# Top-k attention with a squared-ReLU feed-forward: scores laid out with 512 columns in each outer PSUM bank, and half of the pair maxima moved to another bank

## The chip, the cores and the metric

The kernel runs on one core of one Trainium2 chip. A core has a matrix engine (TensorE, "PE" in the profile; its weight loads are listed as "PEld"), a vector engine (VectorE, "DVE"), a scalar engine (ScalarE, "ACT"), a general engine (GpSimd, "POOL") and a queue that issues transfers (SyncE, "SP"). Each engine works through its own list of instructions in order, and the engines wait for one another through semaphores. Matrix products land in PSUM, which this kernel treats as eight banks of 512 fp32 columns on 128 partitions; everything else lies in SBUF.

The metric is device time in microseconds (us): the median over the executions of the program. Lower is better.

## The reference

There are 8 batches of 8 heads; each head has 576 queries and 576 keys of 64 numbers. For every query only the 32 largest scores count. The attention output of all heads, 4608 rows of 512 numbers, then goes through two matrices with a squared ReLU between.

```python
scores = scale * np.matmul(q, k.transpose(0, 1, 3, 2))        # scale = 1/8
kth = np.partition(scores, -top_k, axis=-1)[..., -top_k:-top_k + 1]
scores = np.where(scores >= kth, scores, -1000000000.0)
attn = np.exp(scores - np.max(scores, axis=-1, keepdims=True))
attn = attn / (np.sum(attn, axis=-1, keepdims=True) + 1e-09)
attn_out = np.matmul(attn, v)
x = attn_out.transpose(0, 2, 1, 3).reshape(B * S, H * D)      # 4608 x 512
out = np.maximum(x @ w_in, 0.0) ** 2 @ w_out                  # 512 -> 2048 -> 512
```

## The kernel before

**Blocks.** Two heads form a pair, 32 pairs in all. A *block* is the score table of 128 queries for both heads of a pair: 128 partitions by 2 x 576 columns. A pair has four such blocks, and the last 64 queries of two pairs share a fifth one (the Z block, in which one head's queries lie on partitions 0 to 63 and the other's on 64 to 127). That makes 144 blocks. Each goes through this pipeline, in which some four blocks are under way at a time:

1. *Loads and transposes*, once per pair (`load_pair`). q and k come in by three transfers each (lines 444 and 446), are transposed by PE, and ACT copies them from PSUM into the tile `qk`: 512 columns of q (line 484), 512 of k (line 485), and the remaining 64 of both in one instruction (line 486). In `qk` head 0 of the pair lies on partitions 0 to 63 and head 1 on 64 to 127.
2. *Scores* (`scores`, `scores_z`). The products are fp32. Head 0 uses rows 0 to 63 of the PE array and head 1 rows 64 to 127, so that products of the two can run side by side. Each product is done in two passes, which the profile lists as two matmuls. The 1152 columns of a block lie without a gap in banks 0, 1 and 2: head 0 takes columns 0 to 575, head 1 takes 576 to 1151. [...] head 0 needs products of 512 and 64 columns, and head 1 of 448 and 128. Head 0's 64 columns and head 1's 448 share bank 1; a semaphore (`fence`) keeps the second of them until the first is done.
3. *Copy.* ACT copies the whole block to SBUF, to the tile `st` (line 532).
4. *Pair maxima.* Each row of 576 scores is folded in halves: `m` holds the larger of each pair of scores that lie 288 apart. DVE makes it in two instructions, each taking one operand from PSUM and the other from `st`: `m1` (line 595) for the second half of the pairs, which it writes into PSUM, and `m0` (line 597) for the first half, which goes to SBUF. ACT copies m1's result into `m` (`mc`, line 599). DVE then folds `m` once more into `f` (`big`, line 601), with one operand in PSUM again. POOL makes the smaller members of the pairs by integer sums and differences (line 583).
5. *Selection* (DVE). Rounds of "eight largest" (MAX8, lines 624 and 631) and "strike these out" (MATCH_REPLACE8, line 628) give the 32nd largest score of each row, `kth`.
6. *Mask and probabilities.* ACT turns scores below `kth` into a weight `w` (line 639). In `attend`, PE transposes the nine 128-column parts of a block and adds a steep multiple of `w` to each (`flip`, recorded at the helpers' lines 428 and 425), in a group of four and a group of five; the result `e` takes banks 3, 4 and the first 128 columns of bank 5. One ACT instruction over all three banks makes the exponentials (line 672).
7. *Attention output* (`collect`) and *feed-forward* (`feed`), which uses banks 6 and 7 in turn, as do the transposes of step 1 and the output of step 7.

**Where the pair maxima lie.** m1 writes its 288 columns into columns 128 to 415 of bank 2, beside head 1's last 128 score columns. The scores of the next block begin with a product that covers bank 2, so the plan lets them start only when both the score area (`ss`) and this quarter (`sq`) are free. `ss` comes free after m1, m0 and the copy of line 532; `sq` comes free after `big`, which is its last reader:

```python
pl.op("pe", 1.25 if gi != Z else 1.4, tg - LEAD, scores if gi != Z else scores_z, r=qu,
      w=[ss] + ([sq] if M1 else []), take=[ss, st] + ([sq] if M1 else []))
```

There is one `ss`, one `sq` and one `e` (pools `ps_s`, `ps_q`, `ps_e`, one slot each).

**The order of the work.** Nothing is ordered by hand. The host program describes every operation with an engine, an assumed duration, a priority and its tiles (`Plan.op`); `Plan.schedule` plays the engines through with these durations and gives each free engine the ready operation with the lowest priority number whose tiles are free. The lists that come out are fixed in the program. The constants PER, LEAD, ME, MQ, MP, MA, LAG, STEP, LATE and LAGL are parts of those priorities: PER is the assumed distance of two blocks, LEAD how far ahead scores are made, ME, MQ, MA and MP how early m1/m0, `big`, `mc` and the POOL steps are placed, LAG and LAGL how late the feed-forward is. SQ sets which squares go to POOL and which to ACT (`i * SQ % 8 < SQ`). A tile of a pool is given out in the order in which the tiles were described, except for `psum`, which gives to whoever asks first.

Of the kernel before, what the change touches and what calls it, by code (L numbers as in the profile page):

```python
# [12 lines left out]
P = 128  # L13
# [7 lines left out]
class Pool:  # L21


    def __init__(self, name, n):
        self.name, self.n = name, n
        self.free = list(range(n))
        self.last = [None] * n
        self.made = self.taken = 0

    def take(self, tl):  # L30
        if self.name != "psum" and tl.num != self.taken:
            return None
        s = self.find(tl.width)
        if s is not None:
            self.taken += 1
        return s
# [255 lines left out]
def bass_top_k_attn__then__act_relu_squared_kernel(  # L292
# [11 lines left out]
    REST = (512, 0)  # L304
    NHP = 4
# [8 lines left out]
    def sb(name, shape, dt=FP32, n=None):  # L314
# [4 lines left out]
    PER = 5.5  # L319
    T0 = 12.0  # L320
    LEAD = 25.86
    ME = 12.62
    MQ = 12.73
    MP = 5.72
    MA = 14.76
    SQ = 5.43
    M1 = 1
    LAG = 7.32
    STEP = 3.3
    LATE = 1.21  # L330
    LAGL = 18.31
    WARM = 0
# [22 lines left out]
        "qk": ([P, 2, S], FP32, 5), "vb": ([P, 12, D + 1], BF16, 5),  # L355
# [17 lines left out]
    ps_s, ps_q, ps_e, psum = Pool("ps_s", 1), Pool("ps_q", 1), Pool("ps_e", 1), Pool("psum", 2)  # L373
    BASE = {"ps_s": 0, "ps_q": 2, "ps_e": 3, "psum": 6}
# [13 lines left out]
    def wide(t):  # L388

        b = BASE[t.pool.name]  # L390
        return ps32[:, b:b + 3, :].rearrange("p b c -> p (b c)")[:, 0:2 * S]
# [38 lines left out]
    def build(full, weights, pl):  # L430
# [7 lines left out]
        def load_pair(b, hp, base):  # L438
            rq, rk, rv = tile("rq"), tile("rk"), tile("rv")

            def load(t, src, queue=nc.sync):
                def fn():
                    r = at(t)
                    res = [queue.dma_start(r[:, 0:4, h, :], src[b, 2 * hp + h, 0:512, :].rearrange(
                        "(tb p) d -> p tb d", p=P)) for h in range(2)]
                    res.append(queue.dma_start(
                        r[0:64, 4, :, :], src[b, 2 * hp:2 * hp + 2, 512:576, :].rearrange("h p d -> p h d")))
                    return res
                return fn
# [10 lines left out]
            pl.op("sp", 2.3, base - 80, load(rq, q), w=[rq], take=[rq], sem=slot_sem, ndma=3)  # L460
            via = "act" if not full and not state["pairs"] else None
            state["pairs"] += 1
            pl.op("sp", 2.3, base - 79.9, load(rk, k, nc.scalar if via else nc.sync), w=[rk], take=[rk], sem=slot_sem,
# [12 lines left out]
            def t5():  # L476
# [7 lines left out]
            pl.op("act", .6, base - 42.5, lambda: act.copy(at(qk)[:, 0, 0:512], bank(tq)), r=[tq], w=[qk])  # L484
            pl.op("act", .6, base - 42.4, lambda: act.copy(at(qk)[:, 1, 0:512], bank(tk)), r=[tk], w=[qk])
            pl.op("act", .3, base - 42.3, lambda: act.copy(
                at(qk)[:, :, 512:576], bank(tx)[:, 0:128].rearrange("p (a c) -> p a c", a=2)), r=[tx], w=[qk])
# [4 lines left out]
        def top_k(gi, qks, tg):  # L492
# [6 lines left out]

            def scores():  # L500
                o = wide(ss)
                for h, to, c0, n_ in ((0, 512, 512, 64), (1, 1024, 448, 128), (0, 0, 0, 512), (1, 576, 0, 448)):
                    x = at(qks[h])
                    if to == 576:
                        pe.wait_ge(fence, fences[0])
                    ins = mm(o[:, to:to + n_], x[64 * h:64 * h + 64, 0, 128 * gi:128 * gi + 128],
                             x[64 * h:64 * h + 64, 1, c0:c0 + n_], to != 576)
                    if to == 512:
                        fences[0] += 1
                        ins.then_inc(fence, 1)  # L510
                return ins


            def scores_z():
                o = wide(ss)
                for i, runs in ((0, [((512, 512, 64), (0, 0, 512)), ((512, 0, 64), (0, 64, 512))]),
                                (1, [((1024, 384, 128), (576, 512, 64), (640, 0, 384)),
                                     ((1024, 448, 128), (576, 0, 448))])):
                    x = at(qks[i])
                    for k_ in range(3):  # L520
                        for h in range(2):
                            if k_ < len(runs[h]):
                                to, c0, n_ = runs[h][k_]
                                ins = mm(o[64 * h:64 * h + 64, to:to + n_], x[64 * h:64 * h + 64, 0, 512:576],
                                         x[64 * h:64 * h + 64, 1, c0:c0 + n_], not 576 <= to < 1024)
                return ins

            qu = sorted(set(qks), key=lambda t: t.num)
            pl.op("pe", 1.25 if gi != Z else 1.4, tg - LEAD, scores if gi != Z else scores_z, r=qu,
                  w=[ss] + ([sq] if M1 else []), take=[ss, st] + ([sq] if M1 else []))  # L530

            cp = [pl.op("act", 1.2, tg - LEAD + 1, lambda: act.copy(  # L532
                at(st)[:, :, :].rearrange("p i c -> p (i c)"), wide(ss)), r=[ss], w=[st])]
# [44 lines left out]
            else:  # L578
# [7 lines left out]
                def parts(a, n_):  # L586

                    return two(wide(ss)[:, a:], S, n_), at(st)[:, :, HALF + a:HALF + a + n_]

                def quarter():  # L590
                    return two(ps32[:, 2, 128:416], QUART, QUART)

                if M1:

                    m1 = dve(.36, lambda: vec.tensor_tensor(quarter(), *parts(QUART, QUART), ALU.max), dp=-ME,  # L595
                             r=[ss], hold=[st, sq], after=cp)
                    m0 = dve(.36, lambda: vec.tensor_tensor(at(m)[:, :, 0:QUART], *parts(0, QUART), ALU.max), dp=-ME,  # L597
                             r=[ss], hold=[st], after=cp, w=[m], take=[m])
                    mc = pl.op("act", .45, tg - MA, lambda: act.copy(at(m)[:, :, QUART:HALF], quarter()), hold=[sq],  # L599
                               w=[m], after=[m1, m0])  # L600
                    big = dve(.36, lambda: vec.tensor_tensor(  # L601
                        at(f)[:, :, 0:QUART], at(m)[:, :, 0:QUART], quarter(), ALU.max), dp=-MQ,
                        hold=[m, sq], after=[m0, mc], w=[f], take=[f])
                else:
                    dve(.67, lambda: vec.tensor_tensor(at(m)[:, :, :], *parts(0, HALF), ALU.max), dp=-ME,
                        r=[ss], hold=[st], after=cp, w=[m], take=[m])
                    big = dve(.67, lambda: vec.tensor_reduce(
                        at(f)[:, :, 0:QUART], at(m)[:, :, :].rearrange("p i (a c) -> p i c a", a=2), AX.X, ALU.max),
                        dp=-MQ, r=[m], w=[f], take=[f])
# [45 lines left out]
        def attend(gi, st, wt, tt):  # L655

            e, pt = Tile(ps_e), tile("p")

            def flip(cols, i0):
                sf, wf = (at(t)[:, :, :].rearrange("p i c -> p (i c)") for t in (st, wt))  # L660
                outs = [(wide(e)[:, 128 * (i0 + i):128 * (i0 + i) + 128], c, (i0 + i) % 4 == 0)
# [9 lines left out]
            pl.op("pe", .84, tt + .1, lambda: flip([640, 768, 896, 1024, 512], 4), r=[st, wt], w=[e], order=[o_t])  # L671
            pl.op("act", 1.15, tt + 1, lambda: act.activation(  # L672
                at(pt)[:, :, :].rearrange("p k q -> p (k q)"), wide(e), ACTF.Exp, scale=0.125), r=[e], w=[pt])
# [317 lines left out]
```

## Time and profile before

| | us |
|---|---|
| median of 3 runs (lowest to highest) | 902.43 (901.22 to 904.34) |
| the profiled execution, its own time | 901.76 |
| its span, from the first to the last instruction | 900.0 |
| DVE busy | 830.1 (92% of the span) |
| PE busy | 832.0 (92%) |
| POOL busy | 799.7 (89%) |
| ACT busy | 751.9 (84%) |

A busy engine's time is a union: overlapping instructions are counted once. The durations of single DVE and PE instructions overlap their neighbours, so means times counts exceed the busy time. In a line of instruction groups the figures are: busy us and mean ns of one instruction, then the engine's idle time just before these instructions and what ended most of it. In a list of waits they are: total us, number of waits, longest. In a table of windows each engine has its busy us and its number of instructions, then come the share of full clock that PE was granted, and the share and rate of the DMA engines.

### The profile page before, as it was taken

The numbers are of one execution on the slowest core, as the hardware profiler recorded it, in microseconds if no ns is written. First come the engines' busy times: TensorE is split into PE (matmuls) and PEld (weight loads), VectorE is DVE, ScalarE is ACT, GpSimd is POOL, SyncE is SP. The second block draws the span as 40 slices with busy tenths as digits, with TensorE's granted clock in tenths as the row PEclk, the third lists the DMA queues.
The fourth block names the chain that finished last, engine by engine and source line by source line (L and its number), as shares of the span: only waits on it lengthen the run. The fifth ranks groups of instructions, "written<-read, shape, count | busy, mean of one in ns | idle before, by whom it ended". The sixth has DMA issues, their size and how long they took to land.

```text
span 900.0 us, 21960 instructions
## 1 busy us (share of the span) xinstructions
PE 832.0 (92%) x7810; PEld 598.2 (66%) x7810; DVE 830.1 (92%) x3409; ACT 751.9 (84%) x1210; POOL 799.7 (89%) x833
## 2 busy tenths in 40 slices
PE   5777778999999999998999999999899999999996
PEld 3555556676767666766677657676667676776774
DVE  2988899999999999999999999999999999999961
ACT  3767687898989898989889989898989898888872
POOL 6988898999999899988999999997899999999961
PEclk8988799999999999999999999999999999999999
DMA  6632551101310322012110123202221120000101
GB/s 135 165 109 83 133 117 38 54 9 43 82 39 15 73 71 64 20 39 66 28 52 16 28 63 88 61 13 53 53 57 38 39 54 15 25 2 25 24 14 40
DMA packets 126967, 48.18 MB, mean 54 GB/s; under 512 B 119168, under 2 KB 119168, under 8 KB 126848
## 3 DMA queue, kind: packets, MB, share of 16 engines
q1 hardware_dynamic: 125648, 46.39, 20.6%
q8 instruction: 63, 1.03, 0.5%
q14 instruction: 56, 0.46, 0.2%
q10 hardware_dynamic: 1200, 0.30, 0.2%
HBM read 37.22 MB, written 9.44 MB: 52 GB/s over the span
## 4 chain that ended last, share of the span: by engine, by line
PE 71%; ACT 13%; DVE 12%; issue 1%; DMA 1%; POOL 1%; SPq 0%
PE ps L425 54%; PE ps L428 17%; ACT p L672 4%; ACT s L532 4%; DVE f L628 3%; DVE c L624 3%; DVE kth L631 2%; ACT w L639 2%; DVE f L601 1%; DVE ps L595 1%; DMA rq<-in_q_dram 1%; DVE m L597 1%; ACT m L599 1%; ACT g L752 1%; ACT xt L726 0%
## 5 line engine op out<-in xcount | busy, mean ns | idle before, releaser
L628 DVE MATCH_REPLACE8 f<-c,f 128x104 f32<-128x104 f32 (+2 forms) x864 | 267.8, 316 | 0.0
L425 PE MATMUL ps<-qk 64*128 64x512 f32 (+8 forms) x1312 | 236.4, 455 | 24.5 <-DVE f L601 23.6
L624 DVE MAX8 c<-f 128x8 f32<-128x104 f32 (+2 forms) x864 | 243.4, 320 | 0.0
L639 ACT ACTIVATE w<-s,kth 128x576 bf16<-128x576 f32 x288 | 223.3, 784 | 9.9 <-DVE kth L631 9.6
L583 POOL TENSOR_TENSOR t<-s 128x576 int32<-128x576 int32 x144 | 202.8, 1411 | 29.3 <-ACT s L532 28.9
L532 ACT COPY s<-ps 128x1152 f32<-128x1152 f32 x144 | 161.3, 1120 | 62.9 <-PE ps L425 60.9
L631 DVE MAX8 kth<-f 128x8 f32<-128x576 f32 x288 | 210.4, 750 | 3.2 <-POOL f L583 3.2
L428 PE MATMUL ps<-ident,s 128*128 128x128 f32 x1296 | 199.2, 282 | 9.0 <-ACT p L672 4.9
L583 POOL TENSOR_TENSOR f<-t,m 128x576 int32<-128x576 int32 x144 | 202.8, 1409 | 0.0
L672 ACT ACTIVATE p<-ps 128x1152 bf16<-128x1152 f32 x144 | 163.5, 1136 | 24.7 <-PE ps L425 24.2
L428 PEld LDWEIGHTS ps<-ident,s 128*128 128x128 f32 x1296 | 145.3, 143 | 55.7 <-issue 18.0
L425 PEld LDWEIGHTS ps<-qk 64*128 64x128 f32 (+1 forms) x1312 | 118.7, 179 | 65.0 <-DVE f L601 34.7
L425 PE MATMUL ps<-wo,g 128*128 128x512 bf16 x576 | 143.3, 379 | 0.6 <-ACT xz L727 0.4
L583 POOL TENSOR_TENSOR t<-m 128x288 int32<-128x288 int32 x144 | 114.9, 798 | 21.9 <-ACT m L599 20.7
L425 PE MATMUL ps<-xt,win 128*128 128x256 bf16 (+1 forms) x1088 | 128.7, 267 | 5.3 <-ACT av L698 2.7
L425 PE MATMUL ps<-steep_bf,w 128*128 128x128 bf16 x1296 | 121.5, 222 | 0.0
L583 POOL TENSOR_TENSOR f<-t,f 128x288 int32<-128x288 int32 x144 | 114.8, 797 | 0.7 <-DVE f L601 0.5
L425 PEld LDWEIGHTS ps<-xt,win 128*128 128x128 bf16 x1088 | 95.9, 98 | 26.3 <-ACT av L698 3.3
L763 POOL TENSOR_TENSOR g<-g 128x512 bf16<-128x512 bf16 x95 | 98.4, 1041 | 15.6 <-ACT g L752 14.8
L425 PEld LDWEIGHTS ps<-steep_bf,w 128*128 128x128 bf16 x1296 | 98.3, 99 | 3.6
L595 DVE TENSOR_TENSOR ps<-ps,s 128x288 f32<-128x288 f32 x144 | 66.1, 459 | 36.2 <-ACT s L532 34.8
L752 ACT ACTIVATE g<-ps 128x512 bf16<-128x512 f32 x144 | 85.6, 605 | 9.7 <-PE ps L425 9.2
(57 smaller groups left out, 849.4 us busy)
## 6 DMA issues: line engine op xcount, KB each, us to landing
rq<-in_q_dram SPq DMA_DIRECT2D x64, 128.0 KB, 2.5
rv<-in_v_dram SPq DMA_DIRECT2D x64, 128.0 KB, 2.4
out_dram<-o SPq DMA_DIRECT2D x32, 256.0 KB, 2.3
rk<-in_k_dram SPq DMA_DIRECT2D x62, 128.0 KB, 2.6
g<-in_moe_w_in_dram SPq DMA_DIRECT2D x8, 512.0 KB, 4.1
g<-in_moe_w_out_dram SPq DMA_DIRECT2D x8, 512.0 KB, 4.0
rv<-in_v_dram SPq DMA_DIRECT2D x96, 16.0 KB, 2.2
rq<-in_q_dram SPq DMA_DIRECT2D x32, 32.0 KB, 2.4
```

The costliest lines, as they stand in the source:

```text
L425: return pe.matmul(o, l, r, start=start, stop=stop, skip_group_check=True)
L428: return pe.matmul(o, i, ident, is_transpose=True, skip_group_check=True, **kw)
L532: cp = [pl.op("act", 1.2, tg - LEAD + 1, lambda: act.copy(at(st)[:, :, :].rearrange("p i c -> p (i c)"), wide(ss)), r=[ss], w=[st])]
L583: return pl.op("gp", dur, prio, lambda: gp.tensor_tensor(o().bitcast(I32), x().bitcast(I32), y().bitcast(I32), op), **kw)
L595: m1 = dve(.36, lambda: vec.tensor_tensor(quarter(), *parts(QUART, QUART), ALU.max), dp=-ME, r=[ss], hold=[st, sq], after=cp)
L624: lambda i=i, t=t, c0=c0, c1=c1: vec.max(eighth(t, i), at(f)[:, i, c0:c1]),
L628: lambda i=i, t=t, c0=c0, c1=c1: vec.match_replace(at(f)[:, i, c0:c1], eighth(t, i), at(f)[:, i, c0:c1], NEG), hold=[f])]
L631: ks.append(chain(kth, i, prev[i] + [low], .665, lambda i=i: vec.max(eighth(kth, i), at(f)[:, i, :]), hold=[f]))
L639: pl.op("act", .77, tw + .8 * i, lambda i=i: act.activation(at(wt)[:, i, :], at(st)[:, i, :], ACTF.Relu, bias=kth[:, i, n:n + 1], scale=-1.0),
L672: pl.op("act", 1.15, tt + 1, lambda: act.activation(at(pt)[:, :, :].rearrange("p k q -> p (k q)"), wide(e), ACTF.Exp, scale=0.125), r=[e], ...
L752: return act.activation(at(g)[:, 0:kf * nt], bank(hh)[:, 0:kf * nt], ACTF.Relu)
L763: pl.op("gp", .15 + w_ / 480, tf + lag + 1, lambda g=g: gp.tensor_tensor(at(g)[:, 0:w_], at(g)[:, 0:w_], at(g)[:, 0:w_], ALU.mult), u=[g])
```

## The change

The score area becomes the whole of banks 0, 1 and 2. Head 0 keeps columns 0 to 575; head 1 moves to columns 960 to 1535 (`SECOND` = 960). Banks 0 and 2 are each filled by one product of 512 columns, and bank 1 holds two products of 64 columns, at its two ends. The four products of a block are then 64 (head 0), 512 (head 1), 512 (head 0), 64 (head 1), the last behind the fence. Z blocks have eight products in place of nine. For this, k is kept with its 64 remaining rows at both ends: `qk` is one row of 1216 columns (q 512, q's rest 64, k's rest 64, k 512, k's rest 64 again). For head 1 the rest are k's first 64 rows, not its last; so `load` fetches k's rows 64 to 575 for head 1 and the two rests in one transfer with another stride. ACT fills `qk` with four copies in place of three; the fourth repeats the 64 columns of k's rest.

The quarter of m1 moves to bank 5, columns 128 to 415, behind the last 128 columns of `e`. `ps_q` is now the tile for that bank: m1 takes it (as `sq`) and gives it back after `big`; the ninth flip takes it too (as `e9`) and gives it back after the exponentials. The scores no longer take it. The flips of a block are split into groups of four, four and one. `ps_q` is given to whoever asks first.

`pairs`, which makes m1 and m0, reads head 0's first half and head 1's second half from PSUM (banks 0 and 2), and their counterparts from `st`. The copy of line 532 reads two runs of 576 columns 960 apart. `mc` depends on m1 alone. The branches for M1 = 0 and WARM are deleted, and the constants of the priorities are new.

```diff
     def take(self, tl):
-        if self.name != "psum" and tl.num != self.taken:
+        if self.queue and tl.num != self.taken:
             return None
...
+    SECOND = 3 * 512 - S
...
-    PER = 5.5
+    PER = 5.76
...
-    LEAD = 25.86
-    ME = 12.62
-    MQ = 12.73
-    MP = 5.72
-    MA = 14.76
-    SQ = 5.43
-    M1 = 1
-    LAG = 7.32
-    STEP = 3.3
-    LATE = 1.21
-    LAGL = 18.31
-    WARM = 0
+    LEAD = 26.59
+    ME = 10.33
+    MQ = 12.36
+    MP = 4.03
+    MA = 14.06
+    SQ = 5.68
+    LAG = 17.25
+    STEP = 2.97
+    LATE = 1.59
+    LAGL = 18.87
...
-        "qk": ([P, 2, S], FP32, 5), "vb": ([P, 12, D + 1], BF16, 5),
+        "qk": ([P, 2 * S + 64], FP32, 5), "vb": ([P, 12, D + 1], BF16, 5),
...
-    ps_s, ps_q, ps_e, psum = Pool("ps_s", 1), Pool("ps_q", 1), Pool("ps_e", 1), Pool("psum", 2)
-    BASE = {"ps_s": 0, "ps_q": 2, "ps_e": 3, "psum": 6}
+    ps_s, ps_e, ps_q, psum = Pool("ps_s", 1), Pool("ps_e", 1), Pool("ps_q", 1, False), Pool("psum", 2, False)
+    BASE = {"ps_s": 0, "ps_e": 3, "ps_q": 5, "psum": 6}
...
+                    for h in range(2):
+                        r0 = 64 if h and rest != (512, 512) else 0
+                        res.append(queue.dma_start(r[:, 0:4, h, :], src[b, 2 * hp + h, r0:r0 + 512, :].rearrange(
+                            "(tb p) d -> p tb d", p=P)))
+                    x = src[b, 2 * hp, rest[0]:rest[0] + 64, :]
+                    res.append(queue.dma_start(r[0:64, 4, :, :], bass.AP(
+                        x.tensor, x.offset, [x.ap[0], [(S + rest[1] - rest[0]) * D, 2], x.ap[1]])))
...
-            pl.op("act", .6, base - 42.5, lambda: act.copy(at(qk)[:, 0, 0:512], bank(tq)), r=[tq], w=[qk])
-            pl.op("act", .6, base - 42.4, lambda: act.copy(at(qk)[:, 1, 0:512], bank(tk)), r=[tk], w=[qk])
-            pl.op("act", .3, base - 42.3, lambda: act.copy(
-                at(qk)[:, :, 512:576], bank(tx)[:, 0:128].rearrange("p (a c) -> p a c", a=2)), r=[tx], w=[qk])
+            pl.op("act", .6, base - 42.5, lambda: act.copy(at(qk)[:, 0:512], bank(tq)), r=[tq], w=[qk])
+            pl.op("act", .6, base - 42.4, lambda: act.copy(at(qk)[:, 640:1152], bank(tk)), r=[tk], w=[qk])
+            pl.op("act", .3, base - 42.3, lambda: act.copy(at(qk)[:, 512:640], bank(tx)[:, 0:128]), r=[tx], w=[qk])
+            pl.op("act", .25, base - 42.2, lambda: act.copy(at(qk)[:, 1152:1216], bank(tx)[:, 64:128]), r=[tx], w=[qk])
...
+            RUNS = ((0, 512, 576, 64), (1, 1024, 64, 512), (0, 0, 64, 512), (1, SECOND, 0, 64))
+
             def scores():
-                o = wide(ss)
-                for h, to, c0, n_ in ((0, 512, 512, 64), (1, 1024, 448, 128), (0, 0, 0, 512), (1, 576, 0, 448)):
+                o = banks(ss)
+                for i, (h, to, c0, n_) in enumerate(RUNS):
                     x = at(qks[h])
-                    if to == 576:
+                    if i == 3:
                         pe.wait_ge(fence, fences[0])
...
             def scores_z():
...
+                for i, (blk_, to, c0, n_) in enumerate(RUNS):
+                    x = at(qks[blk_])
+                    for h in range(2):
+                        ins = mm(o[64 * h:64 * h + 64, to:to + n_], x[64 * h:64 * h + 64, 512:576],
+                                 x[64 * h:64 * h + 64, S + c0:S + c0 + n_], i < 3)
                 return ins
...
-            pl.op("pe", 1.25 if gi != Z else 1.4, tg - LEAD, scores if gi != Z else scores_z, r=qu,
-                  w=[ss] + ([sq] if M1 else []), take=[ss, st] + ([sq] if M1 else []))
+            pl.op("pe", 1.37 if gi != Z else 2.1, tg - LEAD, scores if gi != Z else scores_z, r=qu, w=[ss],
+                  take=[ss, st])
 
             cp = [pl.op("act", 1.2, tg - LEAD + 1, lambda: act.copy(
-                at(st)[:, :, :].rearrange("p i c -> p (i c)"), wide(ss)), r=[ss], w=[st])]
+                at(st)[:, :, :], two(banks(ss), SECOND, S)), r=[ss], w=[st])]
...
+                def pairs(o, a):
+                    return vec.tensor_tensor(o, two(banks(ss)[:, a:], SECOND + HALF, QUART),
+                                             two(at(st)[:, 0, HALF + a:], HALF, QUART), ALU.max)
 
                 def quarter():
-                    return two(ps32[:, 2, 128:416], QUART, QUART)
...
+                    return two(bank(sq)[:, P:], QUART, QUART)
+
+                m1 = dve(.36, lambda: pairs(quarter(), QUART), dp=-ME, r=[ss], hold=[st, m], after=cp, w=[sq], take=[m, sq])
+                m0 = dve(.36, lambda: pairs(at(m)[:, :, 0:QUART], 0), dp=-ME, r=[ss], hold=[st], after=cp, w=[m])
+                mc = pl.op("act", .45, tg - MA, lambda: act.copy(at(m)[:, :, QUART:HALF], quarter()), hold=[sq],
+                           w=[m], after=[m1])
+                big = dve(.36, lambda: vec.tensor_tensor(
+                    at(f)[:, :, 0:QUART], at(m)[:, :, 0:QUART], quarter(), ALU.max), dp=-MQ,
+                    hold=[m, sq], after=[m0, mc], w=[f], take=[f])
...
-            e, pt = Tile(ps_e), tile("p")
+            e, e9, pt = Tile(ps_e), Tile(ps_q), tile("p")
...
-            pl.op("pe", .84, tt + .1, lambda: flip([640, 768, 896, 1024, 512], 4), r=[st, wt], w=[e], order=[o_t])
+            o_t = pl.op("pe", .68, tt + .1, lambda: flip([640, 768, 896, 1024], 4), r=[st, wt], w=[e], order=[o_t])
+            pl.op("pe", .2, tt + .2, lambda: flip([512], 8), r=[st, wt], w=[e, e9], take=[e9], order=[o_t])
             pl.op("act", 1.15, tt + 1, lambda: act.activation(
-                at(pt)[:, :, :].rearrange("p k q -> p (k q)"), wide(e), ACTF.Exp, scale=0.125), r=[e], w=[pt])
+                at(pt)[:, :, :].rearrange("p k q -> p (k q)"), banks(e)[:, 0:2 * S], ACTF.Exp, scale=0.125),
+                r=[e, e9], w=[pt])
...
```

## The prediction

> **What bounds the kernel now.** I read the table of windows first, because the shares over the whole span mix a start, a long even middle and an end.
>
> ```profile
> 0.00:150.00 150.00, 108.86 (x884) 76.93 (x884) 121.95 (x497) 100.72 (x155) 125.50 (x152) 0.87 0.48 117
> 150.00:850.00 700.00, 682.42 (x6499) 491.65 (x6498) 684.75 (x2820) 624.06 (x1005) 650.95 (x655) 1.00 0.17 42
> 850.00:900.00 50.00, 40.71 (x432) 29.66 (x428) 23.41 (x94) 27.08 (x51) 23.21 (x27) 0.96 0.07 24
> ```
>
> The columns are PE, weight loads, DVE, ACT, POOL, PE's granted clock and the DMA share. In the middle DVE is busy 684.75 of 700 us (97.8%), and PE 682.42. PE's figure holds the tails of overlapping products, so DVE is the harder limit. DVE's 830.1 us over 144 blocks are 5.76 us a block; the distance from block to block, from the first scores (8.7 us) to the last (849.1), is 840.4 / 143 = 5.88. What can be won is thus DVE's idle time: 28.1 us before 150, 15.3 in the middle, and after 850 another 26.6 in which the last blocks drain. The list of waits says what ended it:
>
> ```profile
> ACT s L532 <- PE ps L425: 60.9, 78, 3.3
> DVE ps L595 <- ACT s L532: 34.8, 40, 12.5
> ...
> PEld ps L425 <- DVE f L601: 34.7, 45, 2.6
> ...
> PE ps L425 <- DVE f L601: 23.6, 23, 2.4
> ...
> DVE f L601 <- ACT m L599: 6.2, 15, 1.1
> ```
>
> These rows close a ring: DVE's L595 waits for the copy L532, that for the scores, the scores for L601, and L601 follows L595. The timeline shows one turn of it, at 98 us:
>
> ```profile
> 97.92 0.44 DVE L601 TENSOR_TENSOR f<-m,ps 128x288 f32<-128x288 f32 x1
> ...
> 98.41 2.60 PE L425 MATMUL ps<-qk 64*128 64x64 f32 x8
> ...
> 101.05 1.12 ACT L532 COPY s<-ps 128x1152 f32<-128x1152 f32 x1 [3.30 <-PE ps L425]
> ...
> 102.20 0.47 DVE L595 TENSOR_TENSOR ps<-ps,s 128x288 f32<-128x288 f32 x1 [1.12 <-ACT s L532]
> 102.57 0.45 DVE L597 TENSOR_TENSOR m<-ps,s 128x288 f32<-128x288 f32 x1
> ...
> 104.53 0.39 ACT L599 COPY m<-ps 128x288 f32<-128x288 f32 x1
> ...
> 104.95 0.46 DVE L601 TENSOR_TENSOR f<-m,ps 128x288 f32<-128x288 f32 x1 [0.46 <-ACT m L599]
> ...
> 105.46 0.71 PEld L425 LDWEIGHTS ps<-qk 64*128 64x128 f32 x5 [0.32 <-DVE f L601]
> ```
>
> From one score group to the next are 7.05 us, and DVE stood idle for 1.12 of them. The eight passes take 2.60 us here, in the stretch with a mean clock of 0.87; at full clock a plain group takes 1.51, one of a Z block 2.17. A turn at full clock: scores 1.51, copy 1.12, L595 and L597 together 0.82, then from the end of L597 to the end of L601 1.62 on average over the 144 blocks, and some 0.15 of hand-offs: 5.2 us of the 5.76 that DVE needs. At 2.60 it is 6.3, and DVE must wait.
>
> **What the change takes out of the ring.** The scores no longer wait for L599 and L601. The ring ends with L597: 1.51 + 1.12 + 0.82 + 0.1 = 3.6 us at full clock, 4.7 in the slow start. Both are under 5.76, so this ring cannot hold DVE any more. What else the moved scores issue is PE work alone, no transfer; on PE they pass feed-forward products and flips, whose readers are ACT's relu and exponentials.
>
> DVE's idle, part by part:
> - *Start.* First L595: 12.5 us. The fourth copy into `qk` stands before the first scores: 64 columns, between nothing and the 128-column copy's 283 ns (L486); by the slope from there to 512 columns (591) some 0.23. So 12.8.
> - *12.5 to 150 us.* Idle 15.5: L595 11.3, L601 4.2. Block by block, the L595 part goes except in block 1 (2.3 idle, scores 0.9 earlier: 1.4 left) and in block 5 (1.8), whose scores wait behind transposes for q's transfer (5.30 us on the chain of waits), which nothing here moves. The L601 part waits for ACT's turn and stays. Left: 3.2 + 4.2 = 7.4.
> - *Middle.* Idle 15.3: L595 12.3, L601 2.9. The scores here began up to 1 us after L601 as often as at once, so PE's own queue holds them too. I take two thirds of the 12.3 as gone; none and all are the ends. Left: 4.1 + 2.9 = 7.0.
> - *End.* The 26.6 us after 850 stay: they are the drain (waits of L760, L700, L631 and L905, 16.7) and 9.9 after DVE's last instruction.
>
> **What it adds.** *Bank 5.* It now has two users in turn. In the trace L595's start to L601's end averages 2.44 us, and the ninth transpose's start to the end of the exponentials 1.87. Here a rule speaks against the change. The row: L672 reads all three banks in one instruction of 1136 ns, though bank 5 holds a ninth of its columns, and the two users' columns do not meet. By columns the two could overlap, and the cost is nil. The Trainium skill, "PSUM — Partial Sum Buffer", section "PSUM bank collisions raise a hardware error", says that two engines must not be in one bank and quadrant at once, whatever the columns. No row here can show a collision, but the plan obeys it: `e9` and `sq` are one tile. By it the holds add up: 2.44 + 1.87 + 0.1 = 4.4 us of 5.76, which fits with 1.3 to spare if the plan places them apart. In the old order they are not apart: 123 times a hold of one kind meets one of the other. In 39 of them L595 would wait for the exponentials, 1.38 us each, 53.8 in sum; behind it on DVE stand L597 and the other block's MAX8s, and for it wait L599 and POOL's small members. In 84 the ninth flip would wait for L601, 1.49 each, 125 in sum; behind it on PE stand the next scores and products, and for it wait the exponentials. The new plan counts these holds, so most such meetings are ordered away. Bounds 0 and 53.8 us on DVE; nearest is the row for the old shared bank, whose ring at 90% of the period left DVE 12.3 idle in 119 middle blocks. At 76% I take 1.5. PE's part lies under DVE's 97.8%; without that cover it would land on the end.
>
> *The score products.* Columns stay 576 for each head, passes eight (Z: 16 for 18). Only the pairing changes: 64 beside 128, then 512 beside 448, becomes 64 beside 512, then 512 beside 64. A rule speaks against this too. The row: in the group at 343.81 us the second pass of head 0's first product starts (343.971) after the first pass of head 1's (343.817); the 512's passes are 0.485 apart and the last pass runs 0.59. The heads advance side by side, so head 0 would need 0.16 + 0.11 + 0.485 + 0.59 = 1.35 us. The Trainium skill, "TensorE: Matmul & The Clock Gate", Part 3 "The mechanism", says that matmuls start and end in strict program order. Taken pass by pass, head 0's 512 would start only after head 1's second 512 pass: 0.16 + 0.485 + 0.05 + 0.485 + 0.59 = 1.78. Over the 128 plain blocks that is -20 or +35 us on PE. The rule's order is not what the row shows for the passes; I take the row's 1.51 as unchanged and keep both ends.
>
> *Edits at nothing.* The fourth copy: 32 x 0.23 = 7 us of ACT, under its 624 of 700 in the middle; it also holds bank 6 or 7 for 0.25 us longer per pair. The ninth flip alone: the same instructions, plus at most its 0.28 us tail where PE has nothing next, under DVE. L532, L595, L597, L601: same elements, same kinds of memory. The three k transfers: same bytes. SQ: 5 of 8 squares on POOL at both values. `mc` free of L597: L597 runs within 0.4 us of L595 in any case. Deleted branches: nothing ran. The new priorities only reorder; LAG puts the feed-forward 10 us later in the middle, LAGL 0.6 at the end.
>
> **Sum.** 12.8 + DVE busy 830.1 + 7.4 + 7.0 + 1.5 + 26.6 = 885.4 us of span, against 12.5 + 830.1 + 15.5 + 15.3 + 26.6 = 900.0. The profiled execution took 901.76, 1.8 more than its span: 887.2. The median, 902.43, lies 0.7 over that execution: 887.9. I say 887.5.
>
> **Rivals.**
> - *Everything idle goes* (20%). Nothing left between first and last block: 12.8 + 830.1 + 26.6 + 1.8 = 871.3; with half of the 15.9 left, 879. For it: both new rings have over 1.2 us of room. Against: the wait for q's transfer and ACT's turns stay. Taken as 876.
> - *PE becomes the bound* (17%). For it: PE's 682 of 700, and the chain that ended last:
>
> ```profile
> PE 71%; ACT 13%; DVE 12%; issue 1%; DMA 1%; POOL 1%; SPq 0%
> ```
>
>   Against: the union counts overlapped tails, and weight loads are busy 491.65 of 700. Half of the +35 us above, half of that uncovered: 887.5 + 9 = 897.
> - *Nothing moves* (6%): the scores start no earlier because PE's queue holds them where L601 did; idle stays at 15.3 and 11 in the start: about 902.
> - *Slower* (7%): bank 5 takes the place of the old wait. Its place is L595 on DVE behind L672, its price 1.38 us a time. From the eleventh such wait on it eats the 14.6 us won; with half of the 39 left (27 us) the time is 902.4 - 14.6 + 27 = 915. Against: the 1.3 us of room.
> - My forecast, 880 to 894, has 50%.
>
> **How the numbers follow.** A difference under 0.3% (899.7 to 905.1) cannot be told from none. Faster: 50 + 20 + 17 = 87%; within 0.3%: 6%; slower: 7%. The range leaves out the last two and the lower third of the first rival, so 873 to 900.
>
> **What would show it.** Right: the waits of PE's L425 for `big` gone as a main row; score groups starting after `m0`, also before `big` ends; L595's idle down from 34.8 to about 22 (12.8 of it the first); DVE's busy unchanged near 830 with over 98.5% in the middle. Bank 5: waits of m1 for the exponentials, of the ninth flip for `big`; few of the first. Score pairing: the time of eight passes against 1.51. Wrong: DVE idle as before with new names in its waits, PE's middle at 99% with DVE's below 97%, or a drain with clearly more or less than 26.6 us of DVE idle.

## The result and the profile after

The changed kernel takes 888.32 us (median of 4 runs, 885.51 to 889.01) where the kernel before, in 4 runs beside it, takes 902.32. The ratio is 0.9837, with a 95% interval of 0.9809 to 0.9864. The forecast was 887.5, with a range of 873 to 900. The profiled execution took 885.51 us, with a span of 883.6; the median lies 2.8 above it.

The table of windows of the changed kernel, in the columns used for the kernel before. The last `big` ends at 839.1 us here, so that is where the drain begins.

```profile
0.00:150.00 150.00, 110.58 (x934) 83.81 (x935) 127.30 (x522) 106.03 (x175) 130.61 (x158) 0.94 0.47 117
150.00:839.00 689.00, 674.19 (x6470) 502.29 (x6469) 682.03 (x2829) 627.17 (x1028) 653.62 (x657) 1.00 0.17 43
839.00:884.00 45.00, 35.24 (x377) 25.61 (x375) 14.69 (x60) 21.27 (x40) 15.06 (x20) 0.94 0.08 27
```

DVE is busy 682.03 of 689 us in the middle, 99.0%, where it was 97.8%. Its idle time there is 7.0 us in place of 15.3. The list of DVE's waits says what went:

```profile
DVE ps L589 <- ACT s L533: 20.1, 10, 12.6
DVE rzall L694 <- ACT av L692: 13.2, 5, 4.4
DVE g L754 <- ACT g L746: 5.0, 4, 3.7
DVE f L599 <- ACT m L597: 4.3, 4, 1.5
DVE f L620 <- POOL f L584: 4.2, 4, 1.9
DVE ps L589 <- ACT p L665: 1.8, 3, 1.4
```

The wait of the pair maxima (L589, m1; the same line records m0) for the copy of the scores fell from 34.8 us in 40 waits to 20.1 in 10, and 12.6 of that is the start. Between 150 us and the last `big` it fell from 11.1 us in 30 waits to 3.7 in 7. The last row is the new one, m1 behind the exponentials in bank 5: 1.8 us, 1.6 of it before 150 us. L694 and L754 belong to the drain. PE's list no longer has the scores' wait for `big` (23.6 us before); its first rows are those of the flips:

```profile
PE ps L427 <- ACT p L665: 27.7, 25, 2.1
PE ps L427 <- DVE f L599: 8.3, 17, 1.1
PE ps L424 <- DVE m L589: 6.7, 9, 1.7
```

The chain that ended last, in which PE had 71% and DVE 12%, is now mostly DVE's:

```profile
DVE 49%; PE 26%; ACT 13%; POOL 6%; issue 5%; DMA 0%; SPq 0%; DVEq 0%; POOLq 0%
```

PE's granted clock in the first 150 us was 0.94 in this profile and 0.87 in the one of the kernel before. DVE's idle time behind the first m1 fell there from 15.5 to 10.1 us, and no run separates how much of that goes with the clock. In the middle the clock is 1.00 in both.

The timeline of one block in the middle (PE, ACT and DVE) shows the new turn:

```profile
355.27 0.43 DVE L599 TENSOR_TENSOR f<-m,ps 128x288 f32<-128x288 f32 x1
...
355.77 0.33 PE L427 MATMUL ps<-ident,s 128*128 128x128 f32 x1
...
356.08 1.34 PE L424 MATMUL ps<-qk 64*128 64x64 f32 x8
356.19 1.13 ACT L665 ACTIVATE p<-ps 128x1152 bf16<-128x1152 f32 x1
...
357.69 1.13 ACT L533 COPY s<-ps 128x1152 f32<-128x1152 f32 x1
...
359.40 0.45 DVE L589 TENSOR_TENSOR ps<-ps,s 128x288 f32<-128x288 f32 x1
...
360.20 0.38 ACT L597 COPY m<-ps 128x288 f32<-128x288 f32 x1
360.42 0.44 DVE L589 TENSOR_TENSOR m<-ps,s 128x288 f32<-128x288 f32 x1
...
360.95 0.43 DVE L599 TENSOR_TENSOR f<-m,ps 128x288 f32<-128x288 f32 x1
```

Three things are to be seen. The copy ends at 358.82 and m1 begins at 359.40: now the copied scores wait for DVE, not DVE for the copy. Over the 144 blocks that distance is 0.56 us on average, where it was 0.14. `mc` (L597) begins before m0, where before it had to follow m0. And the scores of this block still begin after `big` of the block before, because in PE's list the ninth flip, which waits for `big`, stands ahead of them: the scores start before `big` ends in 21 of 143 blocks only.

### The profile page after: what moved, and what is told of

It reads as the page before. It is cut to its first block, busy times and chain, and to the rows that moved or that the text cites. A ratio compares the mean times of both kernels' runs of the same rounds, so it can differ in the third digit from the quotient of the medians.

```text
span 883.6 us, 22178 instructions
## 1 busy us (share of the span) xinstructions
PE 820.0 (93%) x7778; PEld 611.7 (69%) x7778; DVE 824.0 (93%) x3409; ACT 754.5 (85%) x1242; POOL 799.3 (90%) x833
## 4 chain that ended last, share of the span: by engine, by line
DVE 49%; PE 26%; ACT 13%; POOL 6%; issue 5%; DMA 0%; SPq 0%; DVEq 0%; POOLq 0%
PE ps L424 19%; DVE f L620 15%; DVE c L616 12%; DVE kth L623 11%; PE ps L427 7%; DVE ps L589 4%; ACT p L665 4%; DVE f L599 4%; DVE m L589 3%; ACT s L533 3%; ACT w L631 2%; POOL t L584 2%; POOL f L584 2%; ACT g L746 2%; POOL g L757 1%
## 5 line engine op out<-in xcount | busy, mean ns | idle before, releaser
L427 PE MATMUL ps<-ident,s 128*128 128x128 f32 x1296 | 227.0, 285 | 37.7 <-ACT p L665 27.7
L616 DVE MAX8 c<-f 128x8 f32<-128x104 f32 (+2 forms) x864 | 254.0, 323 | 0.0
L424 PE MATMUL ps<-qk 64*128 64x64 f32 (+3 forms) x1280 | 211.9, 450 | 7.4 <-DVE m L589 6.7
L427 PEld LDWEIGHTS ps<-ident,s 128*128 128x128 f32 x1296 | 148.7, 142 | 78.0 <-ACT p L665 36.8
L424 PEld LDWEIGHTS ps<-qk 64*128 64x128 f32 (+1 forms) x1280 | 131.2, 180 | 84.5 <-issue 69.0
L424 PE MATMUL ps<-steep_bf,w 128*128 128x128 bf16 x1296 | 144.8, 221 | 0.0
L424 PEld LDWEIGHTS ps<-steep_bf,w 128*128 128x128 bf16 x1296 | 108.1, 102 | 5.6
L589 DVE TENSOR_TENSOR ps<-ps,s 128x288 f32<-128x288 f32 x144 | 65.2, 453 | 22.2 <-ACT s L533 20.1
```

The costliest lines, as they stand in the source:

```text
L424: return pe.matmul(o, l, r, start=start, stop=stop, skip_group_check=True)
L427: return pe.matmul(o, i, ident, is_transpose=True, skip_group_check=True, **kw)
L589: return vec.tensor_tensor(o, two(banks(ss)[:, a:], SECOND + HALF, QUART), two(at(st)[:, 0, HALF + a:], HALF, QUART), ALU.max)
L616: lambda i=i, t=t, c0=c0, c1=c1: vec.max(eighth(t, i), at(f)[:, i, c0:c1]),
```

## The experiments

Each run changes the changed kernel, except the one marked otherwise. Where nothing else is said, the plan makes a new order of work from the edit. All of them are measured against the kernel before; differences between two of them are differences of medians. The expectations call the new score groups 1.30 us long. That is where the trace lists the end of their last product; the group's longest products end at 1.35 us (1.51 before), and this is the length used below.

The change also gives the plan new assumed durations: of the scores, of the attention output (0.05 + 0.16 n for 0.05 + 0.165 n, n being `nu` in `collect`) and of its transposes (0.03 n + 0.12 for 0.05 n + 0.1). The runs on the priorities leave these durations as they are in the kernel that they start from, and no run prices them by themselves.

**Is it the release of the scores from `big`?** The wait alone is put back:

```diff
-                  take=[ss, st])
+                  take=[ss, st], after=state.get("big", []))
...
+                state["big"] = [big]
```

> The changed kernel with one thing put back: the scores wait for the previous block's big. Ring theory (the gain is the scores' release from big): 898 to 904 us; DVE idle before the pair maxima in the middle back to 10 us or more, PE waits for big of 20 us or more. Product theory (the gain is the shorter score groups, 1.30 us for 1.51): stays at 886 to 892. Constants theory (the gain is the new priorities): the same, 886 to 892.

Measured: 908.90 us, ratio 1.0063 (1.0035 to 1.0092): 20.6 above the changed kernel, although the score groups stay short. So neither the products nor the priorities bring the gain without the release. It is also slower than the ring theory said. DVE's idle in the middle is 26.2 us. Its waits there, from 150 us to the last `big`:

```profile
DVE f L621 <- POOL f L584: 11.4, 13, 2.7
DVE ps L589 <- ACT s L533: 5.1, 8, 2.0
DVE ps L589 <- ACT p L666: 4.9, 13, 1.0
DVE kth L624 <- POOL f L584: 3.0, 2, 2.0
```

The old wait of the pair maxima for the copy hardly comes back: 5.1 us, where the changed kernel has 3.7 and the kernel before 11.1. Here the ring theory, which said 10 or more, failed. Some 12 of the added 19.2 us are waits for POOL's smaller members (14.4 us for 2.5), and nearly 5 are the hand-off of bank 5 (4.9 for 0.2). PE does wait for `big` (35.1 us in the ninth flips, 5.5 in the scores, 26.1 of the two before 150 us). How much the wait costs by itself, apart from the order that the plan makes around it, this run does not show.

**The priorities.** The old ones in the changed kernel:

```diff
-    PER = 5.76
+    PER = 5.5
...
-    LEAD = 26.59
-    ME = 10.33
-    MQ = 12.36
-    MP = 4.03
-    MA = 14.06
-    SQ = 5.68
-    LAG = 17.25
-    STEP = 2.97
-    LATE = 1.59
-    LAGL = 18.87
+    LEAD = 25.86
+    ME = 12.62
+    MQ = 12.73
+    MP = 5.72
+    MA = 14.76
+    SQ = 5.43
+    LAG = 7.32
+    STEP = 3.3
+    LATE = 1.21
+    LAGL = 18.31
```

> The changed kernel with the priorities of the kernel before. Ring theory: 886 to 895, most of the gain stays. Constants theory: 898 or more.

Measured: 898.40 us, 0.9954 (0.9930 to 0.9978). More than half of the gain is gone, so this came out on the constants theory's side. DVE's waits in this run:

```profile
DVE ps L589 <- ACT s L533: 20.5, 11, 12.7
DVE rzall L694 <- ACT av L692: 12.5, 5, 4.3
DVE ps L589 <- ACT p L665: 9.2, 9, 1.9
DVE f L620 <- POOL f L584: 5.5, 9, 1.7
```

The wait for the copy is as short as in the changed kernel (20.5). What came back is the hand-off of bank 5, 9.2 us for 1.8, but 9.0 of it lies before 150 us, where the old priorities do not keep its two users apart. It is not the whole loss: of the 11.5 us that the span is longer, 3.6 are DVE's idle time before 150 us, 4.0 its idle time in the middle (POOL's row is 4.9 there for 2.5), 1.3 the drain and 2.7 DVE's busy time.

The new priorities in the kernel *before*, with nothing else of the change:

```diff
-    PER = 5.5
+    PER = 5.76
...
-    LAG = 7.32
+    LAG = 17.25
...
```

> The kernel before with the new priorities and nothing else. Ring theory: 899 to 915, no gain, and a loss where m1 and big come later while the scores wait for big. Constants theory: 886 to 894.

Measured: 903.72 us, 1.0005 (0.9993 to 1.0017). By themselves they bring nothing. The fourth corner, the wait put back and the old priorities together:

```diff
-    PER = 5.76
+    PER = 5.5
...
-                  take=[ss, st])
+                  take=[ss, st], after=state.get("big", []))
...
```

> The wait for big put back and the old priorities together: the fourth corner beside the changed kernel, the run with the wait back alone and the run with the old priorities alone. If the wait costs its 20 us by itself: 915 to 922. If the release and the new priorities pay only together (the old priorities were made for a schedule with the wait): 898 to 906, so that the wait costs little under the old priorities.

Measured: 909.76 us, 1.0077 (1.0060 to 1.0093), between the two expectations. The four corners, all with the new score columns and bank 5:

| | scores wait for `big` | scores released |
|---|---|---|
| old priorities | 909.76 | 898.40 |
| new priorities | 908.90 | 888.32 |

The release is worth 11.4 us under the old priorities and 20.6 under the new ones. The priorities are worth 10.1 with the release and 0.9 without. The top left corner is 7.3 us slower than the kernel before, so something in the rest of the change costs time as long as the scores wait.

**The score products.** The old columns and products, with the quarter left in bank 5:

```diff
-    SECOND = 3 * 512 - S
+    SECOND = S
...
-            RUNS = ((0, 512, 576, 64), (1, 1024, 64, 512), (0, 0, 64, 512), (1, SECOND, 0, 64))
+            RUNS = ((0, 512, 576, 64), (1, 1024, 448, 128), (0, 0, 64, 512), (1, SECOND, 0, 448))
```

> The changed kernel with the scores in the old columns (head 1 at 576, products 64, 128, 512, 448), and the quarter still in bank 5, so the scores stay released. Score groups back to 1.51 us, 27 us more for PE. Ring theory: 886 to 892, since PE's time lies under DVE's. Product theory: 898 to 904.

Measured: 894.50 us, 0.9911 (0.9885 to 0.9937), between the two. The plan assumes the same durations, so the order of work on every engine is that of the changed kernel. This makes it the cleanest comparison here: 0.16 us more for each of 128 plain score groups (1.51 for 1.35), 20 us of PE and not 27, cost 6.2 us. So PE's time is mostly hidden, not wholly. Since the plan still assumed the shorter groups, I then told it the longer time:

```diff
-            pl.op("pe", 1.37 if gi != Z else 2.1, tg - LEAD, scores if gi != Z else scores_z, r=qu, w=[ss],
+            pl.op("pe", 1.58 if gi != Z else 2.1, tg - LEAD, scores if gi != Z else scores_z, r=qu, w=[ss],
```

> As the run with the old score columns and products, but the plan is told their longer time (1.58 in place of 1.37). If that run was slower than the changed kernel because its plan assumed too short a score group: 887 to 890. If the longer groups themselves cost time: 893 to 896, as before.

Measured: 903.49 us, 1.0005 (0.9989 to 1.0020). Neither expectation foresaw that: the better assumption gave a worse order. The wait of m1 for the exponentials is 10.5 us here, 9.9 of it before 150 us, as under the old priorities; DVE's idle time in the middle is 15.7 us, where the run before had 10.4. A gain of this change can thus be lost by the order of work alone.

**The new columns without the release.** The quarter goes into the free middle of bank 1, so that the scores must wait for `big` and bank 5 has one user. `mc` follows m0 again:

```diff
...
-    BASE = {"ps_s": 0, "ps_e": 3, "ps_q": 5, "psum": 6}
+    BASE = {"ps_s": 0, "ps_e": 3, "ps_q": 1, "psum": 6}
...
-            pl.op("pe", 1.37 if gi != Z else 2.1, tg - LEAD, scores if gi != Z else scores_z, r=qu, w=[ss],
-                  take=[ss, st])
+            pl.op("pe", 1.37 if gi != Z else 2.1, tg - LEAD, scores if gi != Z else scores_z, r=qu, w=[ss, sq],
+                  take=[ss, st, sq])
...
-                    return two(bank(sq)[:, P:], QUART, QUART)
+                    return two(bank(sq)[:, 64:], QUART, QUART)
...
-                           w=[m], after=[m1])
+                           w=[m], after=[m1, m0])
...
```

> The new score columns alone: the quarter lies in the free middle of bank 1, so the scores wait for big as before, and bank 5 has one user. Ring theory: 896 to 904. Product theory: 886 to 892, as score groups keep 1.30 us.

Measured: 912.66 us, 1.0113 (1.0082 to 1.0144), with 31.1 us of DVE idle in the middle. Two rows make up most of it:

```profile
DVE ps L589 <- ACT s L533: 15.1, 20, 1.6
DVE f L620 <- POOL f L584: 12.0, 15, 1.7
```

The short products are worth nothing here. Sharing bank 5 cannot be the whole reason why the waiting versions are slower than the kernel before, since this one doesn't share it. The wait for the copy is back here, other than in the first run. In this one `mc` follows m0, and the stretch from m1's start to `big`'s end is 2.64 us long on average; with `mc` free of m0 and the wait put back it is 2.00.

**Is DVE the bound?** First, `big` done twice, the second time with the same result:

```diff
+                big = dve(.36, lambda: vec.tensor_tensor(
+                    at(f)[:, :, 0:QUART], at(m)[:, :, 0:QUART], quarter(), ALU.max), dp=-MQ,
+                    hold=[m, sq], after=[m0, mc, big], w=[f])
```

> big is done twice, the second time with the same result: about 0.37 us more of DVE a block, 53 us in all. DVE-bound theory: 935 to 950. PE-bound theory: 890 to 905.

Measured: 965.15 us, 1.0696 (1.0665 to 1.0728): 76.8 above the changed kernel, more than either theory gave. DVE's busy time rose by 58.7 to 882.7 us. The rest is idle: 27.0 us in the middle for 7.0. The second `big` also lengthens the hold of bank 5 and delays POOL, so this run mixes two causes. A second one adds DVE work outside that hold, the first MAX8 of one head twice:

```diff
-                    for i in range(2):
+                    for i in (0, 0, 1) if t is c8 else (0, 1):
```

> The first MAX8 of one head is done twice with the same result: DVE work outside the hold of bank 5, about 0.2 us a block, 30 us in all. DVE-bound theory: the time rises by all of it, to 916 to 923. If rings or PE hold the end: under 905.

Measured: 910.82 us, 1.0086 (1.0059 to 1.0113), 22.5 above the changed kernel. The busy row of this run, and that of the changed kernel:

```profile
PE 829.9 (91%) x7778; PEld 616.6 (68%) x7778; DVE 848.8 (93%) x3553; ACT 759.6 (83%) x1242; POOL 801.9 (88%) x833
```

```profile
PE 820.0 (93%) x7778; PEld 611.7 (69%) x7778; DVE 824.0 (93%) x3409; ACT 754.5 (85%) x1242; POOL 799.3 (90%) x833
```

DVE's busy time rose by 24.8 us (0.17 a block, less than the 0.2 that I had assumed, so that the time stays under the range named) and the time by 22.5. Nearly all of it reaches the end: DVE bounds the changed kernel.

**Do the edits costed at nothing cost nothing?** k's rest at one end only, without the fourth copy:

```diff
-            pl.op("act", .25, base - 42.2, lambda: act.copy(at(qk)[:, 1152:1216], bank(tx)[:, 64:128]), r=[tx], w=[qk])
...
-            RUNS = ((0, 512, 576, 64), (1, 1024, 64, 512), (0, 0, 64, 512), (1, SECOND, 0, 64))
+            RUNS = ((0, 512, 0, 64), (1, 1024, 64, 512), (0, 0, 64, 512), (1, SECOND, 0, 64))
```

> k's rest kept at one end only: both of its products read the same columns and the fourth copy falls away, about 9 us of ACT. DVE-bound theory: within 2 us of the changed kernel, 886 to 890. If ACT also holds the end: 880 to 885.

Measured: 887.59 us, 0.9838 (0.9809 to 0.9867). The fourth copy is not needed, as both ends hold the same numbers, and it costs nothing that can be told.

The exponentials in two instructions, for banks 3 and 4 and for bank 5:

```diff
-            pl.op("pe", .2, tt + .2, lambda: flip([512], 8), r=[st, wt], w=[e, e9], take=[e9], order=[o_t])
-            pl.op("act", 1.15, tt + 1, lambda: act.activation(
-                at(pt)[:, :, :].rearrange("p k q -> p (k q)"), banks(e)[:, 0:2 * S], ACTF.Exp, scale=0.125),
-                r=[e, e9], w=[pt])
+            pl.op("pe", .2, tt + .2, lambda: flip([512], 8), r=[st, wt], w=[e9], take=[e9], order=[o_t])
+            pl.op("act", 1.05, tt + 1, lambda: act.activation(
+                at(pt)[:, 0:8, :].rearrange("p k q -> p (k q)"), banks(e)[:, 0:1024], ACTF.Exp, scale=0.125),
+                r=[e], w=[pt])
+            pl.op("act", .35, tt + 1.1, lambda: act.activation(
+                at(pt)[:, 8, :], banks(e)[:, 1024:1152], ACTF.Exp, scale=0.125), r=[e9], w=[pt])
```

> The exponentials of banks 3 and 4 and of bank 5 in two instructions, so that bank 5 is held for a short time and banks 3 and 4 do not wait for the ninth flip. Costs ACT about 25 us. DVE-bound theory: PE's waits for the exponentials fall from 27.7 to under 12, and the time stays at 885 to 892. If the wait for bank 5 holds the end: 875 to 883. If ACT holds it: 895 or more.

Measured: 887.63 us, 0.9836 (0.9798 to 0.9874). The flips' wait for exponentials fell from 27.7 to 3.7 us; the time did not move. But the waiting moved more than it went: the attention products now wait 10.1 us for the second exponentials, and the scores 23.7 for the pair maxima, where they waited 6.7. And of the 27.7 us only 1.8 lay in the middle. So this wait by itself does not set the time; that PE's waiting costs nothing is not shown.

**The drain.** The ninth flip goes back into the second group in the last four blocks:

```diff
+            if state["n"] > NPAIR * NBLK // 2 - 4:
+                pl.op("pe", .84, tt + .1, lambda: flip([640, 768, 896, 1024, 512], 4), r=[st, wt], w=[e, e9], take=[e9],
+                      order=[o_t])
+            else:
...
```

> In the last four blocks the second group has five flips again, as in the kernel before, so that nothing comes between it and the ninth. Theory that the split of the flips lengthens the drain: about 1.2 us less for each of four blocks, 883 to 886, drain (from the last kth to the end) 29 to 31 us in place of 33.7. If the drain has another cause: 887 to 890.

Measured: 885.22 us, 0.9818 (0.9795 to 0.9841). The median is the lowest of all, but the interval overlaps that of the changed kernel. The drain, from the last `kth` to the end, fell only from 33.7 to 32.6 us in the profiles, where the kernel before had 28.4. If the split has a part in it, it is not the main one.

## Why the prediction was right

The total was right: a span of 883.6 us where the sum gave 885.4. Its terms, from the two traces:

| term | predicted | measured |
|---|---|---|
| first L595 (m1) | 12.8 | 12.6 |
| DVE busy | 830.1 | 824.0 |
| idle up to 150 us | 7.4 | 10.1 |
| idle in the middle | 7.0 + 1.5 | 7.0 |
| drain | 26.6 | 29.9 |

**The bound and the ring.** "DVE is the harder limit" holds: added DVE work outside the ring passes to the end nearly whole. The release is necessary: without it no version with the new columns is under 908 us. But the way it works is not the one described. The step "the scores no longer wait for L599 and L601" was read as an earlier start. In most blocks (119 of 143) a ninth flip took the old wait's place in PE's list, and the scores still follow `big`. What did change is the stretch from m1's start to `big`'s end, 1.98 us for 2.44 (m0 comes later in it, `mc` and `big` sooner), and the length of the score groups. So the turn is shorter against DVE's work, and 0.56 us of slack stands where there was 0.14.

The runs side by side say the same. In those where this stretch takes 2.4 us or more, with the scores waiting (before 2.44, new priorities alone 2.51, quarter in bank 1 2.64) or released (`big` twice, 2.62), the pair maxima wait 8.3 to 15.1 us for the copy in the middle. In the other ten it takes 1.89 to 2.16, and they wait 3.0 to 6.6, also where the scores wait for `big`. These runs differ in their order too, so this is a comparison and no proof.

**The score products** were mis-sized. I took 1.51 us as unchanged and gave 1.35 and 1.78 as the ends (the second sum gives 1.77). The groups take 1.35: the lower end, worked out from the row, was right. From a group's start to the copy that waits for it are 1.40 us, where it was 1.54. The strict order of the Trainium skill's page "TensorE: Matmul & The Clock Gate", Part 3, "The mechanism", taken pass by pass, gave the 1.78, and that reading is not what these groups show. Whether whole products end in order the trace cannot tell, as its ends are modelled. The same-order run prices the shorter groups at 6.2 of the 14 us. The rest of the gain was smaller than forecast, so the two errors nearly cancel, and that the total came within 1 us is luck in this part.

**"The new priorities only reorder"** was wrong as a cost of nothing. They are worth 10.1 us with the release; the hand-off of bank 5 (9.2 to 1.8 us) is a part of that, most of it in the start. The 1.5 us taken for this hand-off, in the middle, were near the 1.8 of the whole run only with these priorities. The rival "slower: bank 5 takes the place of the old wait" did not come true, but runs with the release and a less suitable order came to 898 and 903 us (the second with the old products).

**"`mc` free of L597"** was costed at nothing because m0 follows m1 at once. In the new order it doesn't: m0 starts 0.75 us after m1 on average (0.37 before), and `mc` need not wait for it. What this step alone is worth was not tried. The run with the wait put back has it too and takes 908.90 us, so alone it does not bring the gain.

**DVE's busy time** was taken as fixed. It fell by 6.1 us with the same instructions. An instruction that starts after a wait adds more to the busy time than one that follows another closely: m1 advances DVE by 0.466 us after a wait and by 0.37 without one. There were 99 starts after idle time (more than 0.02 us) before and 46 after; 53 times 0.1 makes 5.3 of the 6.1. The twelve runs with the same 3409 DVE instructions bear it out: from 823.0 us of busy time with 39 such starts to 830.9 with 105, which is 0.12 us for each.

**The drain** was said to stay, and DVE's idle time in it grew by 3.3 us. The split flips hold banks 3 and 4 for 5.34 us per block on average, against 4.06 before. In the drain one block's exponentials follow the other's by 4.5 to 5.0 us, with feed-forward products between the parts of the flips, and three blocks' exponentials are still to come after the last `kth`, where it was one. The timeline of the last but one turn (PE and ACT):

```profile
855.69 0.66 PE L427 MATMUL ps<-ident,s 128*128 128x128 f32 x4 [0.36 <-ACT p L665]
...
856.78 0.63 PE L427 MATMUL ps<-ident,s 128*128 128x128 f32 x4
...
857.53 1.06 PE L424 MATMUL ps<-xt,win 128*128 128x128 bf16 x16
...
858.42 0.28 PE L427 MATMUL ps<-ident,s 128*128 128x128 f32 x1
...
859.11 1.12 ACT L665 ACTIVATE p<-ps 128x1152 bf16<-128x1152 f32 x1
...
860.29 0.66 PE L427 MATMUL ps<-ident,s 128*128 128x128 f32 x4 [0.59 <-ACT p L665]
```

The next block's flips cannot begin before these exponentials have read the banks. With five flips in the second group of the last four blocks the last exponentials ended 2.8 us sooner after the last `kth` (12.0 us for 14.8), but the end came only 1.1 sooner, so what sets the drain stays open. In the start, block 1 left more idle than forecast (2.7 us for 1.4), as its score group ran at 2.50 us instead of 1.51; block 5's wait for q's transfer remained on PE (6.0 us) but did not reach DVE.

**Left open:** why the versions with the new columns in which the scores wait are 6 to 11 us slower than the kernel before, why DVE waits for POOL's smaller members in them (12.3 to 19.5 us in the middle, none in the kernel before), and how much of the 20.6 us belongs to the wait itself and how much to the order that the plan makes around it.

## What to carry to other kernels

When two engines are over 95% busy, look for the ring of waits whose turn is nearly as long as the busiest engine's work per step; what can be won by shortening it is about that engine's idle time (here idle fell by 10.3 us in all, and busy time by 6.1 with it). A hit on the total does not confirm the path: put the wait back and see whether the wait that should return does. A shared buffer that replaces a wait is only as good as the order of its users, so the priorities must be fitted again, and the edit should be judged with them, since here neither brought the whole gain without the other. To price a change of one duration, keep the order of work and change only that; a new order can cost more than the thing under test.

## What the runs showed of the hardware

The order of the product sizes changed how long the two heads' products take together. With the same columns per head, at a granted clock of 1.00 the eight passes take 1.35 us as 64, 512, 512, 64 and 1.51 as 64, 128, 512, 448. In the old group at 343.81 us the first long pass starts 0.27 us after the group's beginning, behind the four passes of the two short products. In the new group at 356.08 it starts within 0.01 us, beside the first short one; from there on the long passes start 0.21 to 0.27 apart in both. A short pass that starts later (356.24) is listed as ending before a long one that started earlier (356.51 against 356.78). But ends are modelled: the copy starts 0.10 us after the listed end of the new group's last product and 0.04 after the old one's.

A wait on DVE costs its idle time and about 0.1 us more: m1 takes 0.466 us after a wait and advances DVE by 0.37 without one, and over twelve runs DVE's busy time grows by 0.12 us for each start after idle time.
